# Taking VectorE work out of a recurrence-plus-MLP kernel: a bound moved into another product, a masked copy moved to ScalarE and GpSimd, and an order read from a table

## The chip, the cores and the metric

One core of a Trainium2 chip. The metric is device microseconds for one execution. Three executions of the kernel before took 677.45, 678.53 and 679.85 us; the median is 678.53 us.

## The reference, cut to what matters

```python
# r, k, v, w, a, b: (4, 8, 768, 40), i.e. 32 heads, 768 steps, 40 channels
for t in range(768):                       # per head
    y[t]  = r[t] @ state                   # state: 40 x 40
    Sa    = state @ a[t]
    state = state * w[t] - outer(Sa, b[t]) + outer(v[t], k[t])
x = y.transpose(0, 2, 1, 3).reshape(3072, 320)
out = (((x @ w1) * (x @ w2)) @ w3) @ w_out  # w1, w2: 320 x 1024; w3: 1024 x 1024; w_out: 1024 x 320
```

The MLP weights arrive as 64-bit floats. The decay w lies between 0.85 and 0.95.

## The kernel before, in words

The 768 steps are cut into 12 chunks of 64. The 32 heads form two groups (g = 0, 1) of 8 pairs. For each chunk and group the kernel does the following.

- `load`: SP brings the decays and the b and k vectors into `fm`, and a into `lh`.
- `scale` (L429 to L475): VectorE clamps the decays (f1, L436: minimum with WMAX = 1.5, with the running maximum written to `stats`), then makes their running product with a scan (f2, L441). ScalarE takes Ln and Exp for a first reciprocal `gi` (L445, L448). VectorE refines it by one Newton step (f6, L457: gt = product * gi; f7, L461). Two wide multiplications (f5, L453 and f8, L465) run on VectorE or GpSimd, as the letters in `ON` say.
- `causal` (L490): 64 small matmuls, then ScalarE copies and GpSimd triangular selects (L508).
- `solve`, once per chunk for both groups: a long serial chain on VectorE (from the transposition at L522 through products at L548 and sums at L552 to L597 and L600) inverts the triangular systems. `join` finishes it on TensorE and ScalarE.
- `pairs` (L667, select L677) and `tokens` (L694): more small matmuls with ScalarE copies and GpSimd selects.
- `rec` (L701): the serial part. TensorE multiplies the state (f1, L718), ScalarE copies to `xu`, TensorE makes `hp` (f2, L725), ScalarE copies to `hs`, TensorE multiplies by the solved triangle (f3, L733) into two PSUM banks `us`. Then f4 (L738), four VectorE instructions, writes `us` into `xu`, each multiplied by `mask_h`, a tile that holds -1 where an element is kept and 0 where it is not. TensorE continues with f5 (L745), VectorE scales the new state (L771), TensorE transposes it (L778), ScalarE stores it to `SB`, and L790 writes y. One slot (`rc`) lets a single `rec` run at a time.
- `gather`, then `mlp` (L842 for the first layer, L856 and L859 on its product, L868 for the rest).

Besides this, `convert` (L324 to L341) turns 31 tiles of 64-bit weights into 32-bit ones, with two ScalarE statistics and three VectorE bit operations for each; `product` (L404) multiplies w3 by w_out. The raw tiles go through 4 buffers (`raw`).

The order of the work is made when the program is built. Every step is recorded by `op` with an engine, a cost, a due time, dependencies and buffer slots; `place` (L96 to L197) then plays a greedy list scheduler with these costs, which also picks the buffer of each slot. The result fixes each engine's instruction order: an engine executes its instructions strictly in that order.

Of the kernel before, what the change touches and what calls it, by code (L numbers as in the profile page):

```python
# [1 line left out]

# [59 lines left out]
class Order:  # L62
# [33 lines left out]
    def place(self):  # L96
        ops = self.ops
        for o in ops:
            o["users"], o["wait"] = [], len(o["deps"])
        for o in ops:  # L100
            for d in o["deps"]:
                ops[d]["users"].append(o)
        free = {p: dict.fromkeys(range(n), 0.0) for p, n in SLOTS.items()}
        ready = {e: [] for e in LAT}
        clock, last, lock, dma = {**dict.fromkeys(LAT, 0.0), "pool": 8.0, "dve": 4.0, "sp": 1.0}, None, {"dve": 0.0, "pool": 0.0}, 0.0
        for o in ops:
            o["ready"] = 0.0
            if not o["wait"]:
                ready[o["eng"]].append(o)

        def begin(o):

            t, left = max(o["ready"], clock[o["eng"]]), {}
            for s in o["slots"]:
                if s.at is None:
                    n = left[s.pool] = left.get(s.pool, 0) + 1
                    if len(free[s.pool]) < n:
                        return None
                    t = max(t, sorted(free[s.pool].values())[n - 1])
                else:  # L120
                    t = max(t, s.since)
            if o["two"]:
                t = max(t, lock["pool" if o["eng"] == "dve" else "dve"])
            return t

        uses = {p: {o["eng"] for o in ops for s in o["slots"] if s.pool == p} for p in SLOTS}
        placed, cand, spare = [], {}, {}

        def choice(e, starts):
            if not starts:  # L130
                return None
            first = min(t for t, _ in starts)
            if e != "pe":
                return first, min((o for t, o in starts if t <= first + 1e-9), key=lambda o: (o["due"], o["n"]))
            return min(((t, o) for t, o in starts if t <= first + P["sl"]),
                       key=lambda x: (x[1]["due"] - P["kp"] * (MODE[x[1]["kind"]] == MODE.get(last)) + P["kw"] * (x[0] - first), x[1]["n"]))

        while len(placed) < len(ops):
            best = None
            for e in LAT:  # L140
                if e not in cand:

                    starts, short = [], 1e9
                    for o in ready[e]:
                        t = begin(o)
                        if t is not None:
                            starts.append((t, o))
                        elif e == "pe" and any(s.pool == "bank" and s.at is None for s in o["slots"]):
                            short = min(short, o["due"] + P["mg"])
                    some = [x for x in starts if x[1]["due"] < short or not any(s.at is None for s in x[1]["slots"])]  # L150
                    spare[e] = len(some) < len(starts)
                    cand[e] = choice(e, some)
                if cand[e] and (best is None or cand[e][0] < best[0]):
                    best = cand[e]
            if best is None and any(spare.values()):
                e = "pe"
                best = choice(e, [(t, o) for o in ready[e] if (t := begin(o)) is not None])
            if best is None:
                raise ValueError(f"stuck after {len(placed)} of {len(ops)}")
            t, o = best  # L160
            e = o["eng"]
            ready[e].remove(o)
            stale = {e, *(("dve", "pool") if o["two"] else ())}
            cost = o["cost"]
            if e == "pe":
                if MODE[o["kind"]] != MODE.get(last):
                    cost += DRAIN + LEAD.get(o["kind"], 0.05)
                last = o["kind"]
            for s in o["slots"]:
                if s.at is None:  # L170
                    stale |= uses[s.pool]
                    s.at = min(free[s.pool], key=lambda i: (free[s.pool][i], i))
                    s.since = free[s.pool].pop(s.at)
            clock[e] = t + cost
            if o["two"]:
                lock[e] = clock[e]
            done = clock[e] + LAT[e]
            if e == "sp":
                dma = max(dma, clock[e]) + o["dma"]
                done = dma + LAT[e]  # L180
            o["start"], o["end"] = t, clock[e]
            placed.append(o)
            for s in o["slots"]:
                s.until, s.left = max(s.until, done), s.left - 1
                if not s.left:
                    stale |= uses[s.pool]
                    free[s.pool][s.at] = s.until
            for u in o["users"]:
                u["wait"] -= 1
                u["ready"] = max(u["ready"], clock[e] if u["eng"] == e != "sp" else done)  # L190
                if not u["wait"]:
                    stale.add(u["eng"])
                    ready[u["eng"]].append(u)
            for e in stale:
                cand.pop(e, None)
# [5 lines left out]
def attention_moe(ctx: ExitStack, tc: tile.TileContext, fmx, fma, rv, vt, sq, svr, w12, w12c, w3t, wo, out):  # L201
# [15 lines left out]
    mask_h = cp.tile([128, C + D], F32, name="mask_h")  # L217
    pool.memset(mask_h, -1.0)
    for q in range(2):
        r = slice(64 * q, 64 * q + 64)  # L220
        pool.affine_select(out=mask_h[r, 0:C], in_=mask_h[r, 0:C], pattern=[[1, C]], compare_op=ALU.is_gt,
                           fill=0.0, base=0, channel_multiplier=-1)
# [206 lines left out]
    def scale(c, g, due):  # L429
# [668 lines left out]
```

## Time and profile before

| | |
|---|---|
| median of the runs | 678.53 us |
| profiled execution, span | 676.2 us |
| PE (matmul) busy | 577.7 us, 85% |
| DVE (VectorE) busy | 551.4 us, 82% |
| ACT (ScalarE) busy | 431.8 us, 64% |
| POOL (GpSimd) busy | 211.9 us, 31% |

The profiled execution's own time is known by its span, from the first to the last recorded work, 676.2 us; the median of the timed runs lies 2.3 us above that. Busy times count an instruction from its recorded start to its end, so instructions that overlap on one engine count once. A wait is put down to the instruction that came last. The minimum, median and maximum duration of a line say whether an instruction always takes the same time.

### The profile page before, as it was taken

To read this page: it belongs to the slowest core of one execution; us is meant where nothing else is said; L and a number is where in the kernel's file an instruction comes from. 1 tells how busy PE (TensorE), PEld (TensorE's weight loads), DVE (VectorE), ACT (ScalarE), POOL (GpSimd) and SP (SyncE) were. 2 spreads that over 40 slices of the span, in tenths; PEclk is the share of its full clock that TensorE was granted. 3 is DMA by queue.
4 is the path that set the end of the run, shared out by engine and by line. 5 is a ranking of instruction groups with operands and counts; after the bars stand their busy time and mean duration, and the time that the engine had idled before them with its cause. 6 is when DMAs were issued, how large, how long until landed. Compare 5 with 4: busy or idle time off the path is not lost.

```text
span 676.2 us, 22337 instructions
## 1 busy us (share of the span) xinstructions
PE 577.7 (85%) x9458; PEld 515.3 (76%) x9458; DVE 551.4 (82%) x987; ACT 431.8 (64%) x927; POOL 211.9 (31%) x188
## 2 busy tenths in 40 slices
PE   1422996768799999898999989899999989999996
PEld 1321664556788999788989878789888889898996
DVE  7999999999999799798799798898987997914310
ACT  2886756686776865846837849559578477473321
POOL 4462005233521205505206316245044171120011
PEclk9999997978989999899999999999999999999999
DMA  7954564444214234034133143150341431110101
GB/s 187 245 148 139 169 159 126 132 124 92 60 31 105 69 88 102 14 94 104 33 94 79 32 98 74 42 147 16 83 111 38 99 72 32 45 32 12 34 21 24
DMA packets 61090, 57.56 MB, mean 85 GB/s; under 512 B 29560, under 2 KB 52600, under 8 KB 60984
## 3 DMA queue, kind: packets, MB, share of 16 engines
q1 hardware_dynamic: 60984, 56.07, 32.7%
q8 instruction: 76, 1.25, 0.8%
q14 instruction: 30, 0.25, 0.1%
HBM read 47.40 MB, written 3.93 MB: 76 GB/s over the span
## 4 chain that ended last, share of the span: by engine, by line
DVE 47%; PE 32%; ACT 8%; issue 6%; DMA 4%; POOL 1%; DVEq 0%; SPq 0%; POOLq 0%
PE bank L842 14%; DVE tmp L548 9%; DVE xu L738 6%; PE bank L868 5%; DMA fm<-in_fmx_dram 4%; DVE ab L552 3%; DVE mf L337 3%; ACT JP L212 3%; DVE Tp L552 3%; PE bank L745 2%; DVE fm L441 2%; DVE ab L522 2%; PE bank L725 2%; PE bank L490 2%; DVE w3f L341 2%
## 5 line engine op out<-in xcount | busy, mean ns | idle before, releaser
L842 PE MATMUL bank<-xs,W 128*128 128x256 f32 x1536 | 204.8, 289 | 0.7 <-DVE xs L828 0.7
L842 PEld LDWEIGHTS bank<-xs,W 128*128 128x128 f32 x1536 | 190.3, 193 | 5.8 <-DVE xs L828 0.9
L677 POOL TENSOR_SCALAR_AFFINE_SELECT xu<-xu 64x512 f32<-64x512 f32 x48 | 46.0, 958 | 187.9 <-ACT xu L212 172.1
L212 ACT ACTIVATE xu<-bank 64x256 f32<-64x256 f32 (+2 forms) x184 | 72.6, 437 | 39.4 <-PE bank L718 32.2
L859 POOL TENSOR_TENSOR gl<-ga,gh 128x512 fp32r<-128x512 f32 x32 | 41.0, 1283 | 109.8 <-ACT gh L212 109.8
L212 ACT ACTIVATE JP<-bank 32x512 f32<-32x512 f32 x120 | 60.5, 504 | 22.6 <-PE bank L490 20.7
L490 PE MATMUL bank<-lh,fm 40*64 40x64 f32 x1536 | 32.7, 236 | 45.0 <-POOL fm L465 23.3
L738 DVE TENSOR_TENSOR xu<-bank,mask_h 64x416 f32<-64x416 f32 x96 | 56.3, 587 | 14.0 <-PE bank L733 12.0
L490 PEld LDWEIGHTS bank<-lh,fm 40*64 40x64 f32 x1536 | 29.5, 149 | 49.4 <-POOL fm L465 25.9
L508 POOL TENSOR_SCALAR_AFFINE_SELECT lh<-lh 64x512 f32<-64x512 f32 x48 | 41.0, 853 | 76.8 <-ACT lh L212 73.9
L856 DVE TENSOR_TENSOR ga<-bank,ga 128x512 f32<-128x512 f32 x48 | 32.8, 683 | 39.1 <-PE bank L842 30.3
L868 PE MATMUL bank<-W3h,gh 128*128 128x320 f32 x192 | 63.1, 329 | 1.1 <-DVE xu L738 1.1
L868 PE MATMUL bank<-W3l,gh 128*128 128x320 f32 x192 | 59.2, 309 | 0.0
L868 PE MATMUL bank<-W3h,gl 128*128 128x320 f32 x192 | 59.2, 308 | 0.0
L404 PE MATMUL bank<-wof,w3f 128*128 128x320 f32 x128 | 41.7, 479 | 16.7 <-DVE w3f L341 16.7
L745 PE MATMUL bank<-xu,bk 128*40 128x104 f32 (+1 forms) x768 | 47.5, 262 | 5.9 <-DVE xu L738 5.8
L212 ACT ACTIVATE gh<-ga 128x512 fp32r<-128x512 f32 x48 | 30.3, 631 | 34.6 <-DVE ga L856 34.2
L725 PE MATMUL bank<-xu,lh 128*64 128x104 f32 (+2 forms) x768 | 43.4, 266 | 9.5 <-ACT xu L212 5.8
L453 POOL TENSOR_TENSOR lh<-lh,fm 104x1024 f32<-104x1024 f32 x16 | 35.4, 2216 | 48.4 <-DVE fm L441 22.3
L745 PEld LDWEIGHTS bank<-xu,bk 128*40 128x40 f32 (+1 forms) x768 | 37.5, 120 | 14.7 <-DVE xu L738 12.1
L725 PEld LDWEIGHTS bank<-xu,lh 128*64 128x64 f32 (+2 forms) x768 | 37.6, 144 | 14.2 <-ACT xu L212 6.9
L404 PEld LDWEIGHTS bank<-wof,w3f 128*128 128x128 f32 x128 | 25.8, 210 | 28.7 <-issue 14.3
(99 smaller groups left out, 1190.9 us busy)
## 6 DMA issues: line engine op xcount, KB each, us to landing
fm<-in_fmx_dram SPq DMA_DIRECT2D x24, 627.2 KB
raw<-in_w3t_dram SPq DMA_DIRECT2D x16, 512.0 KB
rv<-in_rv_dram SPq DMA_DIRECT2D x48, 160.0 KB
raw<-in_w_dram SPq DMA_DIRECT2D x8, 512.0 KB
lh<-in_fma_dram SPq DMA_DIRECT2D x48, 80.0 KB
xu<-in_vt_dram SPq DMA_DIRECT2D x48, 80.0 KB
out_dram<-o SPq DMA_DIRECT2D x48, 80.0 KB
xr<-y SPq DMA_DIRECT2D x72, 40.0 KB
```

Of the source, the lines that this page charges most:

```text
L212: act.activation(out_, in_, AF.Copy, scale=scale)
L404: pe.matmul(out=pt.t[:, 0:DM], lhsT=w[:, j], rhs=wof[:, j], start=(j == 0), stop=(j == NJ - 1))
L490: pe.matmul(out=bank(ab)[64 * x:64 * x + 64, p], lhsT=X[r, p, x], rhs=lh.t[r, ab, p], start=True, stop=True)
L508: pool.affine_select(out=lh.t[q, ab], in_=lh.t[q, ab], pattern=[[0, NP], [1, C]], compare_op=ALU.is_gt, fill=0.0, base=0, channel_multipli ...
L548: dve.tensor_tensor(out=scratch(*shape), in0=x().to_broadcast([128, *shape]), in1=y().to_broadcast([128, *shape]), op=ALU.mult)
L677: op("pool", 0.67, due + 2, lambda q=q, ab=ab: pool.affine_select(out=xu.t[q, ab, :, 0:C], in_=xu.t[q, ab, :, 0:C], pattern=[[0, NP], [1, ...
L725: pe.matmul(out=view(hp[h])[64 * ab:64 * ab + 64, u], lhsT=lh.t[k, ab, HP * h + u], rhs=xu.t[k, ab, HP * h + u], start=True, stop=True)
L738: dve.tensor_tensor(out=xu.t[64 * ab:64 * ab + 64, ab, k:NP:2], in0=view(us[ab])[r], in1=mask_h[r].unsqueeze(1).to_broadcast([64, HP, N]), ...
L745: pe.matmul(out=q(r, p), lhsT=bk.t[:, p, r], rhs=xu.t[:, ab, p], start=(c == 0), stop=True, skip_group_check=True)
L842: pe.matmul(out=pt.t[:, TOK * x:TOK * x + TOK], lhsT=WT[k][:, cs], rhs=xs.t[:, z], start=(n == 0), stop=(n == 7))
L859: both(ON["gl"][c % NCH], 1.3, 0.69, t + 1, lambda e, a=a, j=j: e.tensor_tensor(out=gl.t[:, j:j + 2], in0=a.t, in1=gh.t[:, j:j + 2], op=AL ...
L868: pe.matmul(out=pt.t[:, 0:DM], lhsT=l.t[:, j, ts], rhs=W3[r][:, j], start=(j == 0 and n == 0), stop=(j == NJ - 1 and n == 2))
```

## The change

It has three parts.

1. The clamp f1 of `scale` (L436) is gone. The Newton product f6 becomes a scalar_tensor_tensor: minimum of the running product with GMAX = 2^38, times `gi`, with the row sums written to `stats`; the final test compares these sums with NP * C - 0.25 instead of comparing a maximum with WMAX.
2. In `rec`, each of the four VectorE multiplications of f4 becomes a ScalarE copy with scale -1, and two GpSimd selects (f8), one per half `ab`, zero the masked part of the first 64 columns. Each select follows the two copies into its half. `mask_h` and its set-up go.
3. `place` no longer schedules. A table in the source (compressed; two lists, one of the sequence of the steps and one of the buffers of the slots) gives the order; `place` checks it against the dependencies. The steps' costs and due times are still written down, but no longer steer anything. In `convert`, the DMAs of successive tiles are tied to one another in order, as are the first VectorE steps, and f3 must precede the release of the conversion buffers.

The placement letters `ON` and the numbers of buffers `SLOTS` stay as they were.

```diff
-WMAX, GMIN = 1.5, 2.0 ** -40
+GMAX, GMIN = 2.0 ** 38, 2.0 ** -40
-LAT = dict(pe=0.33, act=0.09, dve=0.09, pool=0.1, sp=2.4, nil=0.0)
...
+PLAN = """
...
+"""
     def place(self):
-        ops = self.ops
+        ops, n = self.ops, len(self.ops)
+        code = array("h", zlib.decompress(base64.b85decode("".join(PLAN.split()))))
+        turns, at = list(accumulate(code[:n])), iter(code[n:])
+        assert sorted(turns) == list(range(n))
         for o in ops:
...
             for s in o["slots"]:
                 if s.at is None:
...
+                    s.at = next(at)
+                    assert 0 <= s.at < SLOTS[s.pool]
+        done, holder = set(), {}
+        placed = [ops[i] for i in turns]
+        for o in placed:
+            assert o["deps"] <= done
+            done.add(o["n"])
             for s in o["slots"]:
...
+                h = holder.get((s.pool, s.at))
+                assert h is s or h is None
+                s.left -= 1
+                holder[s.pool, s.at] = s if s.left else None
+        return placed
...
-    mask_h = cp.tile([128, C + D], F32, name="mask_h")
-    pool.memset(mask_h, -1.0)
...
+    pool.memset(stats[:, NCH * NG:2 * NCH * NG], float(NP * C))
...
-        op("sp", 0.35, due - 8, f1, w=[raw], dma=2.5)
+        op("sp", 0.35, due - 8, f1, w=[raw, "turn"], dma=2.5)
         op("act", 0.8, due, f2, r=[raw], w=[sq])
-        op("act", 0.76, due, f3, w=[sq])
-        op("dve", 0.42, due, f4, r=[raw], w=[mf], two=True)
+        op("act", 0.76, due, f3, r=["conv"], w=[sq])
+        op("dve", 0.42, due, f4, r=[raw], w=[mf, "turns"], two=True)
...
-        def f1():
-            w = fm.t[:, 0:NP * W65]
-            dve.tensor_scalar(out=w, in0=w, scalar1=WMAX, scalar2=None, op0=ALU.min, op1=ALU.max,
-                              accum_out=stats[0:104, NCH * NG + i:NCH * NG + i + 1])
...
         def f6():
-            dve.tensor_tensor(out=gt.t, in0=gam(c, g)[:, :, 1:W65], in1=gi.t, op=ALU.mult)
+            dve.scalar_tensor_tensor(out=gt.t, in0=gam(c, g)[:, :, 1:W65], scalar=GMAX, in1=gi.t, op0=ALU.min, op1=ALU.mult,
+                                     accum_out=stats[0:104, NCH * NG + i:NCH * NG + i + 1])
...
-        op("dve", 0.7, due, f1, w=[G])
...
         def f4(ab, x):
             r, k = slice(64 * x, 64 * x + 64), ab ^ x
-            dve.tensor_tensor(out=xu.t[64 * ab:64 * ab + 64, ab, k:NP:2], in0=view(us[ab])[r],
-                              in1=mask_h[r].unsqueeze(1).to_broadcast([64, HP, N]), op=ALU.mult)
+            copy(xu.t[64 * ab:64 * ab + 64, ab, k:NP:2], view(us[ab])[r], -1.0)
+
+        def f8(ab):
+            u = xu.t[64 * ab:64 * ab + 64, ab, :, 0:C]
+            pool.affine_select(out=u, in_=u, pattern=[[0, NP], [1, C]], compare_op=ALU.is_gt, fill=0.0, base=0,
+                               channel_multiplier=-1)
...
         for ab, x in QUADS:
-            op("dve", 0.6, due + 5, lambda ab=ab, x=x: f4(ab, x), r=[us[ab]], w=[(xu, "u", ab, x)])
+            op("act", 0.521, due + 5, lambda ab=ab, x=x: f4(ab, x), r=[us[ab]], w=[(xu, "u", ab, x)])
+        for ab in range(2):
+            op("pool", 0.67, due + 5.5, lambda ab=ab: f8(ab), w=[(xu, "u", ab, 0), (xu, "u", ab, 1)])
```

## Rows read from the trace of the kernel before

**Rows 1.** The windows view, four stages: length, busy us (instructions) by engine, clock, DMA.

```profile
core 0: us, PE busy (x) PEld busy (x) DVE busy (x) ACT busy (x) POOL busy (x), PEclk, DMA share, GB/s
0.00:75.00 75.00, 26.00 (x392) 20.50 (x392) 68.75 (x107) 48.18 (x117) 31.47 (x40) 1.00 0.66 177
75.00:200.00 125.00, 100.07 (x1561) 78.93 (x1564) 118.10 (x232) 89.59 (x203) 40.34 (x33) 0.90 0.41 111
200.00:600.00 400.00, 381.50 (x6747) 348.57 (x6740) 346.33 (x619) 270.25 (x565) 132.31 (x109) 0.99 0.30 72
600.00:677.00 77.00, 70.10 (x773) 67.36 (x771) 18.26 (x31) 23.74 (x45) 7.76 (x6) 0.98 0.09 21
sum 677.00, PE 577.66 PEld 515.35 DVE 551.44 ACT 431.76 POOL 211.88; mean PE 144.42 PEld 128.84 DVE 137.86 ACT 107.94 POOL 52.97
```

**Rows 2.** The page's chain that ended last, share of the span by engine.

```profile
DVE 47%; PE 32%; ACT 8%; issue 6%; DMA 4%; POOL 1%; DVEq 0%; SPq 0%; POOLq 0%
```

**Rows 3.** What SP's queue waited for: us in total, times, longest.

```profile
SPq L324 <- DVE w3f L341: 47.6, 15, 6.9
...
SPq L324 <- DVE wof L341: 17.7, 5, 5.6
```

**Rows 4.** Durations by line, ns minimum/median/maximum: the clamp, f6 and f7.

```profile
L436 DVE TENSOR_SCALAR_CACHE_REDUCE fm<-fm x24: 669/694/696, 7.4 to 547.7; 104x520 f32<-104x520 f32 x24
L436 DVE DVE_READ_ACCUMULATOR fm<-fm x24: 81/83/88, 8.0 to 548.3; 104x1 f32 x24
...
L457 DVE TENSOR_TENSOR gt<-fm,gi x24: 654/693/1701, 11.3 to 554.0; 104x512 f32<-104x512 f32 x24
...
L461 DVE SCALAR_TENSOR_TENSOR gi<-gt,gi x24: 677/693/1025, 12.2 to 555.3; 104x512 f32<-104x512 f32 x24
```

**Rows 5.** The windows view of L436 alone (count with its accumulator reads).

```profile
0.00:75.00 75.00, 2.76 (x8) 1.00 0.66 177
75.00:200.00 125.00, 2.79 (x8) 0.90 0.41 111
200.00:600.00 400.00, 11.22 (x32) 0.99 0.30 72
```

**Rows 6.** The windows view of L738 alone.

```profile
75.00:200.00 125.00, 9.39 (x16) 0.90 0.41 111
200.00:600.00 400.00, 42.23 (x72) 0.99 0.30 72
```

**Rows 7.** Groups by shape, busy us and mean ns: L738, a like ScalarE copy.

```profile
L738 DVE TENSOR_TENSOR xu<-bank,mask_h 64x416 f32<-64x416 f32 x96 | 56.3, 587 | 14.0 <-PE bank L733 12.0
...
L212 ACT ACTIVATE xu<-bank 64x416 f32<-64x416 f32 x44 | 20.1, 506 | 32.5 <-PE bank L718 32.2
```

**Rows 8.** GpSimd's durations by line, ns minimum/median/maximum: selects, then the wide multiplications.

```profile
L677 POOL TENSOR_SCALAR_AFFINE_SELECT xu<-xu x48: 652/828/1859, 37.4 to 593.6; 64x512 f32<-64x512 f32 x48
...
L508 POOL TENSOR_SCALAR_AFFINE_SELECT lh<-lh x48: 649/660/1522, 19.4 to 563.8; 64x512 f32<-64x512 f32 x48
...
L453 POOL TENSOR_TENSOR lh<-lh,fm x16: 2176/2195/2556, 9.5 to 549.7; 104x1024 f32<-104x1024 f32 x16
...
L465 POOL TENSOR_TENSOR fm<-fm,gi x12: 2337/2368/2802, 34.9 to 556.1; 104x1024 f32<-104x1024 f32 x12
```

**Rows 9.** The timeline of one rec step: start, length, engine and line.

```profile
609.24 0.94 PE L733 MATMUL bank<-hs,TT 64*64 64x104 f32 x32
...
610.30 2.45 DVE L738 TENSOR_TENSOR xu<-bank,mask_h 64x416 f32<-64x416 f32 x4 [5.98 <-PE bank L733]
...
613.02 1.63 PE L745 MATMUL bank<-xu,bk 128*40 128x104 f32 x32
```

**Rows 10.** What PE waited for between 200 and 600 us: total, times, longest.

```profile
PE bank L490 <- POOL fm L465: 3.8, 2, 2.7
...
PE bank L745 <- DVE xu L738: 1.4, 6, 0.3
...
PE bank L694 <- DVE xu L738: 0.9, 1, 0.9
```

More of the change, by code (lines that the diff above doesn't have):

```diff
@@ L1 @@
+import base64
+import zlib
+from array import array
 from contextlib import ExitStack
+from itertools import accumulate
 import concourse.bass as bass
@@ new lines @@
+IuX8LmoSN(^ObLCT^`ybGWmLl#!Msmxj8r#SkX$k~W|YSlfTCqJGuDH_j~@@i2!r<qg${=1Da85pnPp8Zsi=5tHQN0%wT=BK6HS@O^|SU#2v6{X+Fpml+^
+Q!jCSXRy2f;XR+DE%b&Iql-G9U(|<zkWcX(g>i8-mIsUI9bM>Io+%!uOk;PwMT@8>Q1NfQhZoT_IfFC#(dsJ-bj+t@xd1#}qlGjay{}VY_+vWv!;YghoeF
+6Nt%Gk$@dj$EC#4Eqq&c*KzQVe!H>n{XlA7F7`@@ocy@yWY>mc1kBjn$dPsj6US;JlA2Cc#R(<GgeXaww(A67b}i+QBR>Np-FmCaD?sPEDleTY)&8>zvnM
+<hUJWH;t6jCCf`<2c0wW*Al~!{10O{R@^*iqnV9aa)wGP>c@d4{5tC$+vX|C2Ag6ekzrsZkmYwj@H*TLsqe$+G!2`##S(iI#^P;o0jDhb_M^co9QQegKG2
+3x*cPB>UwG`6M3LKZ;r|xS<HXoR0`YtZ2!-6)RHutF4$4rMjiw*mh)`tu5DxqcJQJ`Q=0VS1(L3n%*&c4w_%55DQ$kV_tO=9)SR>fc@15*kD0T!xH)b6@~
@@ new lines @@
+3px#?tTlq+xjTq)ml?8UZ^i;G0-V*K+g=zMVtwbM}TlhHD(``51b4*AY^XN}zQL^ZjW{nzHnTy${c&!Q@1&%JjOvL!ESnjO6#}TRWFifRy6qTRWR)$#71R
+;$|B?g?W#einbWAc#r7>U&Yd3eg|i~*Zj*qY&z={dDyt8?`>ss-WD@Q?R_+a7s)Lh#7m_Y`)HQ9k@JDqzC2e7qPP1#fCIFIZd%nLyqSK4^$gAy3%r%W4pU
+`3PJalNoFn;67yX1%Xs;}x8}@P7?k&2Hnrn*m=2d8AX$xIKZ|DZPpq=zEjiRo&=b>7htPONAEtl@xTWdgX7E>Rs31l)=)9&0C?bo%hR_DXwzC=?6{uWqYM
+>FU<*kT<`kz?ROC8)w&T0pV#9TYIi{3NMh<ON+UztC!Gud9IGL~X09$&aTp8e>N2Ogbjzz}_h1r|+c#&MJCLN^>+Fg<^?bv%gSvz6MLANoOuX{V~fGeN!f
+ID)rC>(9ry*nXZG%<imZnjNuvBbpumN6&7z~_USO-z=xHi=(-)pX_SdK(<H{AgFS3&KvDKnMVrT1JB+7e{A`c^*K7eZQ0JoMu2*bfGXV3r=Qm)_{N|D!&-
@@ new lines @@
+3y0v23Hsa){h@DwsG8K6(*~x0#;Td6b~nwJ|r<k$PMA09S><zf>9qjs5}lEP!40*ZKIxV28<=?YvFm+T0ozZL6*)1J`Msf)OKR2ENp>eoA4h!=;2-PxWmI
+50QO9=+~m~(bKlJX^Zo$rjDAW@v_Hc*k5tpJK%GI4wKrZ6|S=p8y3+h9Zyqq96Ymx3ej<$rVDVNLK(I_Ptiq)afRrlu94H=X(8;bxlYlFeA5o%^T5xKG7%
+@tvH^3$o~E);g{E4Z<^c_F13SHRHt?{VW{Qv6@no&c-${9R`<g9iuG<3CoL7MzEue_4buC3<?}nN{bv8&|^OARcSwEG={0Y4TJX?(tGL2y~605>KxvK4W2
+hi+nmu|=K0r0^2;<9aEe$ZaJ6m7?}i}oJVU6*_Q?5VA_GFaP9+d-M8NMZUMYjx8$Tm>_{g&w!<0Ni_mGq-GB(^cPwHq4cQyo{VmB!QdPZGN100I%@S(G_0
+H&=vHTt!kRW#vjvJ?W)tI2j5GLI8jgQD^TgTVRc3OtgT`y>q&YJ{r;mRpm4is2jbybeM9T(Xq?_ay?a7Cp9Q~`(rVcQhQH>ia6ZIaM*pX|6Exljh3kM(Px
@@ L52, in __init__ @@
     def __init__(self, order, pool):
-        self.order, self.pool, self.at, self.left, self.since, self.until = order, pool, None, 0, 0.0, 0.0
+        self.order, self.pool, self.at, self.left = order, pool, None, 0
         if order.direct:
@@ L96, in place @@
     def place(self):
-        ops = self.ops
+        ops, n = self.ops, len(self.ops)
+        code = array("h", zlib.decompress(base64.b85decode("".join(PLAN.split()))))
+        turns, at = list(accumulate(code[:n])), iter(code[n:])
+        assert sorted(turns) == list(range(n))
         for o in ops:
[L99 to L113, printed above, removed]
             for s in o["slots"]:
                 if s.at is None:
[L116 to L168, printed above, removed]
-            for s in o["slots"]:
[L170 to L195, printed above, removed]
@@ L216, in attention_moe @@
     make_identity(nc, ident)
-    mask_h = cp.tile([128, C + D], F32, name="mask_h")
-    pool.memset(mask_h, -1.0)
[L219 to L222, printed above, removed]
     first = cp.tile([104, NP, W65], F32, name="first")
@@ L472, in scale @@
         both(ON["lh"][c], 2.2, 1.22, due + 1, f5, r=[G], w=[(lh, 0), (lh, 1)])
-        op("dve", 0.71, due + 2, f6, r=[G, gi], w=[gt], two=True)
+        op("dve", 0.78, due + 2, f6, r=[G, gi], w=[gt], two=True)
         op("dve", 0.73, due + 2, f7, r=[gt], w=[gi], two=True)
@@ L1013, in attention_moe @@
     dve.tensor_scalar(out=stats[:, 0:n1], in0=stats[:, 0:n1], scalar1=0.5 / GMIN, scalar2=None, op0=ALU.is_lt)
-    dve.tensor_scalar(out=stats[:, n1:2 * n1], in0=stats[:, n1:2 * n1], scalar1=WMAX, scalar2=None, op0=ALU.is_lt)
+    dve.tensor_scalar(out=stats[:, n1:2 * n1], in0=stats[:, n1:2 * n1], scalar1=NP * C - 0.25, scalar2=None, op0=ALU.is_gt)
     dve.tensor_scalar(out=stats[:, 2 * n1:2 * n1 + NCH], in0=stats[:, 2 * n1:2 * n1 + NCH], scalar1=0.0, scalar2=0.0,
```

42 lines of the change are left out of this document (38 added, 4 removed).

## The prediction

> **What bounds the kernel now.** I read the windows view first, cut into four stages, because the shares of the whole span hide that the limit changes. The reader should compare TensorE's and VectorE's busy times with each stage's length. In the first 75 us VectorE is busy 68.75 and TensorE only 26.00; from 75 to 200 us VectorE is busy 118.10 of 125 and TensorE 100.07; from 200 to 600 us TensorE is busy 381.50 of 400 and VectorE 346.33; after 600 us TensorE works off the last MLPs almost without a gap, 70.10 of 77 [rows 1]. So VectorE sets the pace of the head and TensorE that of the rest. Since TensorE's work (577.66 us) is the same before and after, the span is this work plus TensorE's idle time: 49.0 us before 75, 24.9 from 75 to 200, 18.5 from 200 to 600, 6.1 from there to the end at 676.2. The change can only win what it takes out of these 98.5 us.
>
> Next the chain that ended last: VectorE has 47% of it, TensorE 32%, DMA only 4% [rows 2]. To see whether the head is short of data, I then looked at what SP's queue waits for. It waits for VectorE's last conversion step to free a raw buffer, 47.6 us on the w3 tiles and 17.7 us on the wo tiles [rows 3]: the transfers stand behind VectorE, not VectorE behind the transfers. That is my main reason to count VectorE time saved in the head as time saved.
>
> **The clamp that goes into f6.** It removes 24 instructions of 0.694 us, 16.8 us in all [rows 4, 5]; the accumulator read of 0.083 us that follows each lies mostly inside it. Of these 2.76 + 2.79 = 5.55 us lie in the first 200 us and 11.22 in the next 400. The new f6 is not in the trace. From below: f7 has the same kind of instruction and the same size, and its median is that of the old f6, 0.693 us [rows 4], so the extra cost is nothing; it can't be less, since the elements are as many. From above: one accumulator read each, 24 x 0.083 = 2.0 us. I take the upper end because the new f6 has an accumulator: 8 x 0.083 = 0.7 us of it in the head.
>
> **The masked copy that leaves VectorE.** 96 instructions of 0.587 us go, 56.3 us [rows 7]; 9.39 us of them lie between 75 and 200 us and 42.23 between 200 and 600 [rows 6]. ScalarE gets 96 copies. One of the same shape, from PSUM to the same tile, takes 0.506 us [rows 7], so 48.6 us in all and 72 x 0.506 = 36.4 us between 200 and 600, where ScalarE rises from 270.25 to 306.7 us of 400 [rows 1]. TensorE's MLP backlog covers them; if that cover went, each rec step would show its copies as TensorE idle time, some 2.0 us. GpSimd gets 48 selects of 64 x 512 elements, which cost between 0.652 us (shortest) and 0.828 us (median of L677, the same tile) [rows 8]: 31 to 40 us on an engine that is busy 211.88 us. I price its occupancy at nothing, because GpSimd has over 260 us free between 200 and 600.
>
> What counts is the longer way from L733 to L745. Now it is four VectorE instructions in 2.45 us, and TensorE fills it: L733 ends at 610.18 and L745 begins at 613.02, 0.27 us after the last masked copy ends at 612.75 [rows 9]. Afterwards the four copies take 4 x 0.506 = 2.02 us; the third completes half 0 at 1.52 us, and two selects in a row end at 1.52 + 2 x 0.652 = 2.82, or 1.52 + 2 x 0.828 = 3.18 us. That is 0.37 to 0.73 us later than 2.45, so 0.10 to 0.46 us past the present filler; on the 18 steps (72 / 4) between 200 and 600 this makes 1.8 to 8.3 us. I take 0.15 us each, 2.7 us, nearer to the lower end, because TensorE usually has another MLP group at hand.
>
> A wait is also added: the selects queue on GpSimd, strictly in order, behind whatever stands there, and L745 then waits for them, and the state, the next rec step and the gather for L745. The things that stand there are the wide multiplications of 2.2 to 2.4 us [rows 8]. I price this at nothing in the forecast and as a rival below.
>
> In exchange four waits of TensorE for L738 between 200 and 600 us vanish: 1.4 at L745, 1.3 at L667, 1.1 at L868 and 0.9 at L694, together 4.7 us (the first and the last are shown) [rows 10]. What comes late next is the causal matmul waiting for the wide multiplication on GpSimd, 3.8 us [rows 10]; I leave it as it is. So this stage wins 4.7 - 2.7 = 2.0 us.
>
> **The order from a table.** What it holds can't be read from the source, so I bound it. In the head, VectorE loses 5.55 + 9.39 - 0.7 = 14.3 us. If the order stayed as it is, that is the gain. The upper end is all of TensorE's idle time between 75 and 200 us, 24.9: between 200 and 600 VectorE falls from 346.33 to 346.33 - 11.22 - 42.23 + 1.3 = 294.2 us of 400 (16 f6 reads are the 1.3), so an order may push the solves of later chunks out of the head and bring the conversions and the first MLP forward, and the freed room is 106 us. I take the middle, 19.6, since nothing in the trace favours either end. A bad order can also lose; that is not limited from below by any row, and is in the rivals. TensorE's clock is a further unknown: its mean is 0.90 between 75 and 200 us, 1.00 before and 0.99 after [rows 1]. With its two levels, 2.4 and 1.2 GHz, this means a fifth of the 125 us, 25 us, on the lower one, worth at most 12.5 us if denser work there keeps the higher one, and as much lost if that share doubles. I take nothing.
>
> The `convert` dependencies add no work; the tied DMAs go through SP's queue alone, where they went in one queue already. The removed set-up of `mask_h` runs on GpSimd before its first work and I price it at nothing.
>
> **Sum.** 676.2 - 19.6 - 2.0 = 654.6 us of span. The median of the runs lies 2.3 us above the profiled span, so I forecast 656.9, rounded to 657 us.
>
> **GpSimd and VectorE hold one another up.** The same instruction on the same shape varies: the select L677 takes 0.652 to 1.859 us [rows 8], the old f6 0.654 to 1.701 us [rows 4], f7 0.677 to 1.025 us [rows 4]. The long cases fit a conflict between the two engines. The Trainium skill (SBUF — State Buffer, Who interferes with whom) says that a VectorE instruction with two SBUF inputs and a GpSimd instruction that reads SBUF exclude one another for the whole instruction, and that one with at most one SBUF input does not take part. By that rule, with which these ranges agree, L738 (one input in PSUM) disturbed nobody, while each new select may stop a solve step: the rule speaks against the change.
>
> **The rivals.** (a) The conflict costs most of the gain. Of the head's relief 8 selects take up to 0.828 us each back, 6.6 us, which leaves 7.7, and I grant the order nothing more; between 200 and 600 the way through ScalarE and GpSimd is at its upper end, 8.3 - 4.7 = 3.6 us lost. 676.2 - 7.7 + 3.6 + 2.3 = 674 us. For it: the spread of durations. Against it: only 8 of the selects lie in the head.
>
> (b) The order is much better than the old one. TensorE's idle time after 75 us is 43.4 us up to 600; the forecast takes 21.6 of it, and half of the remaining 21.8 gives 657 - 10.9 = 646 us. For it: the 106 us that VectorE has free in the middle. Against it: the head's conversions still all need VectorE.
>
> (c) Slower: the selects come late on GpSimd. If a wide multiplication (2.3 us) stands before the selects in every second of the 24 rec steps and the rest of the way is at its upper end, TensorE loses 12 x 2.3 + 24 x 0.46 = 38.6 us, against 19.6 + 4.7 = 24.3 us won: 676.2 + 14.3 + 2.3 = 693 us. It decides from a mean uncovered wait of 24.3 / 24 = 1.0 us for each step. For it: the written cost of a select is 0.67 us, and the median of L677 is 0.828, so an order made with that cost would come out late. Against it: 28 multiplications spread over the span leave GpSimd mostly idle.
>
> (d) The change doesn't do what it says: VectorE gets free, but the first solves and conversions end no earlier since the table places them no earlier. Then the time stays at about 678 us. For it: half of TensorE's idle time lies before 75 us, where no L738 is. Against it: rows 3.
>
> **How the numbers follow.** Forecast 0.58, (a) 0.14, (b) 0.14, (c) 0.10, (d) 0.04. A measurement of this kernel can tell 0.3%, 2 us, from no change. Faster: the forecast, (b) and nearly all of (a), 0.85. Within 0.3%: (d) and the edge of (a), 0.05. Slower: (c), 0.10. The range runs from 641 us (into the better half of (b)) to 677 us, past (a); below it lies about 0.06 and above it 0.14. The likeliest case alone runs from 648 to 667 us.
>
> **What would show it.** L436 and L738 are gone, and VectorE is busy about 480 us (551.4 - 71). TensorE's idle time between 75 and 200 us has fallen to about 5 us, and the first L842 comes some 20 us earlier. Between 200 and 600 TensorE stays above 380 of 400 us. The chain has less of VectorE. Wrong would be: TensorE waiting at L745 for GpSimd's selects for over 10 us in total (c); f6 well over 0.8 us or solve steps longer than before (a); the 49.0 us of idle time before 75 us cut strongly, which I count as fixed.

## The result, and the profile after

The changed kernel takes 650.7 us (median of 649.08 to 652.73, 4 runs), beside 677.99 us before (4 runs of the same comparison). The ratio is 0.9593, with a 95% interval of 0.9563 to 0.9624: faster by 4%, 27 us. The forecast was 657 us, 641 to 677. The profiled execution, the slowest of the four, has a span of 651.0 us, 25.2 less than before. Ratios leave out slow executions, over 1.5% above the fastest of their kernel; in the whole record that is one, 662.23 us in a second series of the changed kernel (after_again), which the median given there leaves out too.

The windows view of the changed kernel, columns as in [rows 1]:

```profile
0.00:75.00 75.00, 23.34 (x446) 19.36 (x447) 66.76 (x106) 47.05 (x112) 30.44 (x38) 0.84 0.61 173
75.00:200.00 125.00, 105.88 (x1650) 86.62 (x1651) 103.13 (x212) 103.58 (x238) 53.44 (x44) 0.89 0.42 121
200.00:600.00 400.00, 391.04 (x6994) 360.47 (x6998) 289.15 (x534) 305.42 (x649) 151.74 (x146) 1.00 0.30 71
600.00:652.00 52.00, 43.44 (x386) 42.65 (x374) 10.34 (x18) 14.24 (x26) 6.53 (x6) 0.94 0.09 23
sum 652.00, PE 563.70 PEld 509.11 DVE 469.39 ACT 470.28 POOL 242.15; mean PE 140.92 PEld 127.28 DVE 117.35 ACT 117.57 POOL 60.54
```

The reader should again take TensorE's busy time from the length of each stage. Its idle time is 51.7 us before 75, 19.1 from 75 to 200, 9.0 from 200 to 600 and 7.6 to the end, 87.3 us in all, where [rows 1] give 49.0, 24.9, 18.5 and 6.1. So 11.2 us of the 25.2 are idle time, 5.8 of it between 75 and 200 us and 9.5 between 200 and 600; the other 14.0 us come from the busy time itself, which fell from 577.66 to 563.70 us though the matmuls are the same 9458. VectorE is busy 469.39 us instead of 551.44. The chain that ended last, which had 47% of VectorE [rows 2], now reads:

```profile
PE 57%; DVE 5%; ACT 5%; DMA 3%; POOL 2%; issue 2%; SPq 0%; DVEq 0%; ACTq 0%; POOLq 0%
```

The durations of the new f6 with its accumulator read, and of the new selects (ns, minimum/median/maximum), answer to [rows 4] and [rows 8]:

```profile
L423 DVE SCALAR_TENSOR_TENSOR gt<-fm,gi x24: 655/698/1332, 10.2 to 533.8; 104x512 f32<-104x512 f32 x24
L423 DVE DVE_READ_ACCUMULATOR gt<-fm,gi x24: 72/77/84, 11.4 to 534.4; 104x1 f32 x24
...
L708 POOL TENSOR_SCALAR_AFFINE_SELECT xu<-xu x48: 651/657/1971, 86.7 to 603.5; 64x512 f32<-64x512 f32 x48
```

The first MLP matmul, before (L842) and after (L814): the view by line gives the first and the last start in us behind the durations.

```profile
L842 PE MATMUL bank<-xs,W x1536: 276/282/582, 169.5 to 662.7; 128*128 128x256 f32 x192
```

```profile
L814 PE MATMUL bank<-xs,W x1536: 276/282/562, 159.8 to 635.9; 128*128 128x256 f32 x192
```

It comes 9.7 us earlier, and the last one 26.8 us earlier. TensorE's waits before (first row) and after (total, times, longest):

```profile
PE bank L745 <- DVE xu L738: 5.8, 16, 1.2
```

```profile
PE bank L375 <- ACT sq L298: 22.5, 1, 22.5
...
PE bank L715 <- POOL xu L708: 13.6, 9, 5.8
```

The first of the two rows after is one long gap while the first weights are converted (the product at L375); it lies in the 51.7 us. The selects hold TensorE up at L715 (which was L745) for 13.6 us; before, VectorE's masked copy did so for 5.8 us. One rec step of after, the counterpart of [rows 9]:

```profile
599.70 0.94 PE L699 MATMUL bank<-hs,TT 64*64 64x104 f32 x32
...
600.77 1.58 ACT L188 ACTIVATE xu<-bank 64x416 f32<-64x416 f32 x3 [0.31 <-PE bank L699]
601.88 0.66 POOL L708 TENSOR_SCALAR_AFFINE_SELECT xu<-xu 64x512 f32<-64x512 f32 x1 [9.74 <-ACT xu L188]
...
602.89 0.51 ACT L188 ACTIVATE xu<-bank 64x416 f32<-64x416 f32 x1
...
603.48 0.70 POOL L708 TENSOR_SCALAR_AFFINE_SELECT xu<-xu 64x512 f32<-64x512 f32 x1 [0.94 <-ACT xu L188]
...
604.55 1.63 PE L715 MATMUL bank<-xu,bk 128*40 128x104 f32 x32
```

L699 (which was L733) ends at 600.64 and L715 begins at 604.55: the order leaves 3.9 us between them, where [rows 9] left 2.84. Worked out in this way from the timelines for all 24 steps, the mean is 4.1 us after and 2.8 before (2.82; 3.32 in kept_both, the first of the experiments).

### The profile page after: what moved, and what is told of

The parts are those of the page before. It is cut to its first block, busy times and chain, and to the rows that moved or that the text cites. A ratio compares the mean times of both kernels' runs of the same rounds, so it can differ in the third digit from the quotient of the medians.

```text
span 651.0 us, 22281 instructions
## 1 busy us (share of the span) xinstructions
PE 563.7 (87%) x9458; PEld 509.1 (78%) x9458; DVE 469.4 (72%) x867; ACT 470.3 (72%) x1023; POOL 242.2 (37%) x234
## 4 chain that ended last, share of the span: by engine, by line
PE 57%; DVE 5%; ACT 5%; DMA 3%; POOL 2%; issue 2%; SPq 0%; DVEq 0%; ACTq 0%; POOLq 0%
PE bank L814 23%; PE bank L840 11%; PE bank L691 4%; PE bank L715 4%; PE bank L456 3%; PE bank L750 2%; ACT xu L188 2%; PE bank L699 2%; DMA fm<-in_fmx_dram 2%; PE bank L660 2%; PE bank L684 2%; PE bank L596 2%; DVE tmp L514 1%; PE bank L589 1%; ACT JP L188 1%
## 5 line engine op out<-in xcount | busy, mean ns | idle before, releaser
L814 PE MATMUL bank<-xs,W 128*128 128x256 f32 x1536 | 204.1, 286 | 0.6 <-DVE xs L800 0.2
L814 PEld LDWEIGHTS bank<-xs,W 128*128 128x128 f32 x1536 | 187.7, 189 | 6.1 <-DVE xs L800 0.4
L188 ACT ACTIVATE xu<-bank 64x416 f32<-64x416 f32 (+2 forms) x280 | 124.1, 463 | 55.9 <-PE bank L684 20.9
L708 POOL TENSOR_SCALAR_AFFINE_SELECT xu<-xu 64x512 f32<-64x512 f32 x48 | 40.7, 847 | 128.7 <-ACT xu L188 122.8
L188 ACT ACTIVATE JP<-bank 32x512 f32<-32x512 f32 (+1 forms) x120 | 59.4, 501 | 9.1 <-PE bank L456 4.2
L831 POOL TENSOR_TENSOR gl<-ga,gh 128x512 fp32r<-128x512 f32 x32 | 43.2, 1352 | 60.4 <-ACT gh L188 53.1
L474 POOL TENSOR_SCALAR_AFFINE_SELECT lh<-lh 64x512 f32<-64x512 f32 x48 | 36.0, 750 | 68.1 <-ACT lh L188 66.8
L643 POOL TENSOR_SCALAR_AFFINE_SELECT xu<-xu 64x512 f32<-64x512 f32 x48 | 38.9, 812 | 58.0 <-ACT xu L188 56.3
L375 PE MATMUL bank<-wof,w3f 128*128 128x320 f32 x128 | 39.7, 461 | 23.7 <-ACT sq L298 22.5
L715 PE MATMUL bank<-xu,bk 128*40 128x104 f32 (+1 forms) x768 | 44.5, 267 | 13.8 <-POOL xu L708 13.6
L456 PEld LDWEIGHTS bank<-lh,fm 40*64 40x64 f32 x1536 | 28.3, 149 | 33.1 <-issue 20.4
L715 PEld LDWEIGHTS bank<-xu,bk 128*40 128x40 f32 (+1 forms) x768 | 37.7, 124 | 19.8 <-POOL xu L708 17.2
L375 PEld LDWEIGHTS bank<-wof,w3f 128*128 128x128 f32 x128 | 24.4, 198 | 33.8 <-ACT sq L298 22.6
L691 PE MATMUL bank<-xu,lh 104*64 104x104 f32 (+2 forms) x768 | 45.0, 271 | 5.8 <-ACT xu L188 4.7
L691 PEld LDWEIGHTS bank<-xu,lh 104*64 104x64 f32 (+2 forms) x768 | 38.9, 147 | 10.5 <-ACT xu L188 6.7
L407 DVE TENSOR_TENSOR_SCAN fm<-fm,first 104x520 f32<-104x520 f32 x24 | 31.0, 1292 | 18.8 <-DMA fm<-in_fmx_dram 18.5
```

The lines of the kernel that those rows point to most:

```text
L188: act.activation(out_, in_, AF.Copy, scale=scale)
L375: pe.matmul(out=pt.t[:, 0:DM], lhsT=w[:, j], rhs=wof[:, j], start=(j == 0), stop=(j == NJ - 1))
L456: pe.matmul(out=bank(ab)[64 * x:64 * x + 64, p], lhsT=X[r, p, x], rhs=lh.t[r, ab, p], start=True, stop=True)
L474: pool.affine_select(out=lh.t[q, ab], in_=lh.t[q, ab], pattern=[[0, NP], [1, C]], compare_op=ALU.is_gt, fill=0.0, base=0, channel_multipli ...
L643: op("pool", 0.67, due + 2, lambda q=q, ab=ab: pool.affine_select(out=xu.t[q, ab, :, 0:C], in_=xu.t[q, ab, :, 0:C], pattern=[[0, NP], [1, ...
L691: pe.matmul(out=view(hp[h])[64 * ab:64 * ab + 64, u], lhsT=lh.t[k, ab, HP * h + u], rhs=xu.t[k, ab, HP * h + u], start=True, stop=True)
```

## The experiments

Four kernels separate the new instructions from the new order. Eight more runs look at the selects, at what a freed VectorE is worth and at how much the changed kernel itself varies. Each diff is cut to the lines that matter. The table holds more than the order: it also picks the buffers, and the new dependencies in `convert` come with it. No run separates these from the order, so "the table" below means all of it.

**New instructions, old order (kept_both).** The scheduler of before plans as before; only what each step issues differs. f6 and f8 are those of the change.

```diff
         def f1():
-            w = fm.t[:, 0:NP * W65]
-            dve.tensor_scalar(out=w, ...)
+            pass
...
         def f4(ab, x):
-            dve.tensor_tensor(out=xu.t[...], in0=view(us[ab])[r], in1=mask_h[r]..., op=ALU.mult)
+            copy(xu.t[64 * ab:64 * ab + 64, ab, k:NP:2], view(us[ab])[r], -1.0)
+            if (ab, x) in ((0, 1), (1, 0)):
+                f8(ab)
```

> The order of before, step for step, with the new instructions: no clamp, f6 with its accumulator, the masked copy on ScalarE and GpSimd at the place in the order where VectorE had it. Theory 1 (the relief of VectorE and the order each give about half): VectorE's 14.3 us in the head come off and the longer way to L745 costs 1 to 5 us, so 660 to 668 us. Theory 2 (it is the order that pays, the relief alone is soaked up): within 3 us of before, 675 to 681. Theory 3 (it is the relief alone): 648 to 654, as after.

Measured: 696.95 us, ratio 1.0279 (1.0238 to 1.0321). All three theories missed: the new instructions in the old order are 19 us slower than before. What waited for whom, before and in kept_both (total, times, longest):

```profile
DVE y L790 <- PE bank L745: 1.4, 2, 1.2
...
DVE st L771 <- PE bank L745: 0.8, 2, 0.6
```

```profile
POOL xu L738 <- ACT xu L212: 164.0, 25, 30.5
...
DVE st L771 <- PE bank L745: 62.3, 36, 7.0
...
PE bank L745 <- POOL xu L738: 25.6, 32, 4.1
```

TensorE waits 25.6 us for the selects, 1.07 us for each of the 24 steps, and VectorE stands 62.3 us before the scaling of the state (L771), which comes behind L745. GpSimd is mostly idle ahead of the selects: in 25 waits it stands 164.0 us until ScalarE's copies are done. Two stages, columns as in [rows 1]:

```profile
75.00:200.00 125.00, 92.12 (x1390) 71.75 (x1389) 101.45 (x194) 92.21 (x211) 44.62 (x40) 0.90 0.40 110
200.00:600.00 400.00, 378.06 (x6674) 345.15 (x6677) 297.99 (x538) 300.63 (x625) 145.18 (x139) 0.99 0.30 72
```

From 75 to 200 us VectorE is busy only 101.45 us (118.10 before [rows 1]) and TensorE has lost, not won: 92.12 against 100.07. The timeline of that stage shows why (start, length, engine and line; in brackets the idle time before and what ended it):

```profile
153.85 0.65 POOL L738 TENSOR_SCALAR_AFFINE_SELECT xu<-xu 64x512 f32<-64x512 f32 x1
...
154.56 0.57 PE L745 MATMUL bank<-xu,bk 128*40 128x104 f32 x2 [4.14 <-POOL xu L738]
155.04 0.66 POOL L738 TENSOR_SCALAR_AFFINE_SELECT xu<-xu 64x512 f32<-64x512 f32 x1 [0.54 <-POOL xu L738]
...
155.76 3.00 PE L745 MATMUL bank<-xu,bk 128*40 128x104 f32 x30 [0.63 <-POOL xu L738]
157.40 0.32 DVE L771 TENSOR_TENSOR st<-bank,fm 104x160 f32<-104x160 f32 x1 [2.80 <-PE bank L745]
...
159.36 0.68 DVE L336 SCALAR_TENSOR_TENSOR mf<-raw,mf 128x512 uint32<-128x512 uint32 x1
```

TensorE stands 4.14 us until the first select; VectorE can't scale the state until 157.40; and a weight conversion (L336) that stands behind it in VectorE's order begins only at 159.36. The first MLP matmul starts at 178.6 us, 9.1 later than before:

```profile
L842 PE MATMUL bank<-xs,W x1536: 276/282/582, 178.6 to 680.0; 128*128 128x256 f32 x192
```

**New instructions, the greedy scheduler (greedy_both).** The kernel before with both instruction changes of the diff, planned anew by its own `place`.

```diff
-        op("dve", 0.7, due, f1, w=[G])
...
-        op("dve", 0.71, due + 2, f6, r=[G, gi], w=[gt], two=True)
+        op("dve", 0.78, due + 2, f6, r=[G, gi], w=[gt], two=True)
...
-            op("dve", 0.6, due + 5, lambda ab=ab, x=x: f4(ab, x), ...)
+            op("act", 0.521, due + 5, lambda ab=ab, x=x: f4(ab, x), ...)
+        for ab in range(2):
+            op("pool", 0.67, due + 5.5, lambda ab=ab: f8(ab), ...)
```

> Both instruction changes, and the greedy scheduler of before makes the order anew with their costs; no table. Theory 1: between before and after, 658 to 668 us, a little better than the kept order. Theory 2 (the table's order pays): 670 or more. Theory 3 (the relief alone): 648 to 656.

Measured: 701.78 us, 1.035 (1.0309 to 1.0391), which of the three theories only theory 2's "670 or more" covers. The old scheduler, told of the new costs, does no better than the old order.

**The table with old instructions (table_mask_old, table_all_old).** The changed kernel, first with the masked copy back on VectorE and empty select steps, then with the clamp in front of the scan and the plain f6 too.

```diff
-            copy(xu.t[64 * ab:64 * ab + 64, ab, k:NP:2], view(us[ab])[r], -1.0)
+            dve.tensor_tensor(out=xu.t[...], in0=view(us[ab])[r], in1=mask_h[r]..., op=ALU.mult)
...
-            op("act", 0.521, due + 5, lambda ab=ab, x=x: f4(ab, x), ...)
+            op("dve", 0.6, due + 5, lambda ab=ab, x=x: f4(ab, x), ...)
...
-            op("pool", 0.67, due + 5.5, lambda ab=ab: f8(ab), ...)
+            op("pool", 0.67, due + 5.5, lambda: None, ...)
```

> The table's order with the clamp change kept, but the masked copy back on VectorE with the mask and no select. VectorE gets 56 us more, ScalarE 49 and GpSimd 41 less. Theory 1: VectorE is short of time again in the head and nearly so in the middle: 658 to 668 us. Theory 2: within 4 us of after, 647 to 655. If the way over ScalarE and GpSimd is what costs (13.6 us of TensorE's waits for the selects), it is even faster than after: 640 to 648.

> The table's order with all the old instructions: clamp, plain f6, masked copy on VectorE. Theory 1: some 4 to 8 us above the same with the new clamp, 664 to 674 us. Theory 2 (the order pays): 648 to 658. Theory 3 (the relief alone): as before, 674 to 681.

Measured: 700.12 us, 1.0307 (1.0259 to 1.0355), and 717.24 us, 1.0591 (1.0538 to 1.0643). Every theory missed again: the table alone is worth nothing, it loses 39 us with the old instructions. VectorE is on the path again: it has 45% of the chain that ended last in table_mask_old, against 5% after.

```profile
DVE 45%; PE 31%; ACT 8%; DMA 7%; issue 6%; POOL 2%; SPq 0%; DVEq 0%; ACTq 0%; POOLq 0%
```

The 24 clamps, 16.8 us of VectorE [rows 5], cost 717.24 - 700.12 = 17.1 us, though that run also saves the 1.9 us of the new f6's accumulator reads; by the two ratios it is 19 us, give or take 5. The 96 masked copies, 56.3 us [rows 7], cost 700.12 - 650.7 = 49.4 us; this is not VectorE's time alone, since the same edit takes the copies off ScalarE, the selects off GpSimd and changes the way to L715. Two of TensorE's waits in table_mask_old are for VectorE's scaling of the state (1.9 us after) and, where the changed kernel waits 13.6 us for the selects, for the masked copy:

```profile
PE bank L752 <- DVE st L745: 18.0, 17, 2.3
PE bank L717 <- DVE xu L710: 16.3, 15, 4.2
```

**VectorE's wait filled with other work (kept_later).** As kept_both, with up to 3 us of solve steps pulled in front of each scaling of the state and each y.

```diff
+                room, j = 3.0, i + 1
+                while j < len(line) and room > 0:
...
+                        if o["n"] in self.steps:
+                            line.insert(i, line.pop(j))
+                            i, room = i + 1, room - o["cost"]
```

> As kept_both, and on VectorE alone up to 3 us of the solve steps that stand behind each scaling of the state and each y are pulled ahead of them. Theory A (VectorE, freed, reaches the scaling of the state too early and stands there in order until L745 is done: 62 us of waits in kept_both): these waits fall below 35 us and the time to 672 to 687. Theory B (the loss is TensorE's wait for the selects at L745, 25.6 us in kept_both, and VectorE's wait is only its shadow): 692 to 700, as kept_both.

Measured: 765.77 us, 1.1309 (1.1259 to 1.1359), far outside both theories. VectorE's wait at this place fell to 36.1 us, but now TensorE waits for the scaling:

```profile
PE bank L799 <- DVE st L792: 38.9, 19, 7.0
PE bank L765 <- POOL xu L758: 22.8, 30, 3.8
```

The first row is a wait that kept_both hardly had; the second is nearly what it was. Where VectorE was early, it is now late. It also stands 57.5 us for the transfers into `fm` (10.1 in kept_both), so the shift moved more than one wait; which of them costs how much of the 69 us isn't separated.

**The selects in the table's order (zero_select, zero_noselect, zero_memset).** The copies scaled by 0, then no selects, then memsets in their place.

```diff
-            copy(xu.t[64 * ab:64 * ab + 64, ab, k:NP:2], view(us[ab])[r], -1.0)
+            copy(xu.t[64 * ab:64 * ab + 64, ab, k:NP:2], view(us[ab])[r], 0.0)
...
+            pool.memset(xu.t[64 * ab:64 * ab + 64, ab, :, 0:C], 0.0)    # zero_memset alone, as f8
```

> After, with the masked copies scaled by 0 in place of -1, so that what the next two runs leave out can't blow the numbers up. The recurrence's own product is lost, the time should not change: 648 to 654 us.

> As zero_select, without the 48 selects on GpSimd. If TensorE's 13.6 us of waits for them are on the path, 636 to 644 us; if the table's order has covered them, 647 to 653.

> As zero_select, with a memset of the same elements on GpSimd in the place of each select: a write without a read. If what selects cost is the conflict of two engines' reads, this is as fast as without selects, within 2 us; if it is the longer way to L745, as slow as with them, within 2 us.

Measured: 652.51 us with selects (ratio 0.9598 to 0.9701), 647.79 without (0.9521 to 0.9598), 648.29 with memsets (0.9514 to 0.9618). By the medians the selects cost 4.7 us with the table; the two ratios, 0.965 and 0.9559, differ by 6 us, and their intervals leave anything from about 2 to 10. By the medians a write without a read costs nothing and the read all of it, but the intervals of memset and select overlap, so this stays open. The durations are clear, in zero_select and in zero_memset:

```profile
L708 POOL TENSOR_SCALAR_AFFINE_SELECT xu<-xu x48: 652/659/1977, 86.3 to 599.8; 64x512 f32<-64x512 f32 x48
```

```profile
L707 POOL MEMSET xu<- x48: 516/520/528, 87.3 to 598.4; 64x512 f32 x48
```

The select takes up to three times its shortest time, the memset always the same within 12 ns. Laid over VectorE's instructions in the trace of zero_select, 17 of the 18 selects of over 0.72 us overlap one that reads two SBUF tiles (23 of the 30 short ones do, too, so the overlap alone does not lengthen them); 38 of the 48 memsets overlap such an instruction, and none is longer for it.

**Old order without the selects (kept_noselect).** As kept_both, scale 0, no selects.

```diff
-            copy(xu.t[64 * ab:64 * ab + 64, ab, k:NP:2], view(us[ab])[r], -1.0)
-            if (ab, x) in ((0, 1), (1, 0)):
-                f8(ab)
+            copy(xu.t[64 * ab:64 * ab + 64, ab, k:NP:2], view(us[ab])[r], 0.0)
```

> As kept_both, with the copies scaled by 0 and no selects (so the recurrence's own product is lost): the order of before, the relief of VectorE, and no longer way over GpSimd. Theory B (kept_both loses by TensorE's waits for the selects at L745, 25.6 us against 5.8 before): the waits go and the relief comes out, 662 to 676 us. Theory C (an order made for the old durations gains nothing from a freed VectorE, in any case): 677 to 690.

Measured: 678.37 us, 1.0002 (0.9968 to 1.0035), the time of before. Theory B is right on the loss: without the selects the 18.6 us are gone. It is wrong on the rest: the relief does not come out, and theory C's range holds. VectorE has 63 us less work (488.49 busy), and the first MLP matmul starts at 174.2 us, 4.7 later than before. The waits at L738 (which was L745):

```profile
DVE st L764 <- PE bank L738: 37.0, 31, 6.3
...
DVE y L783 <- PE bank L738: 11.0, 4, 9.7
```

```profile
PE bank L738 <- ACT xu L212: 9.9, 16, 1.2
```

The first two are 48 us in which VectorE stands in order; before, L771 and L790 waited 2.2 us there. The third is TensorE's wait for the copies, which in this run are still on ScalarE: 9.9 us, against 5.8 for VectorE's masked copy before. So the run shows what the relief is worth together with the copies on ScalarE, not what it would be worth alone.

**VectorE time out of the head, nothing added (before_less_convert).** The kernel before without f5 of `convert`, one VectorE instruction for each tile. f4 gets other constants and takes 0.497 us in the mean for 0.433, so that VectorE's busy time falls by 20.4 us (551.4 to 531.0).

```diff
-            dve.tensor_scalar(out=mf.t, in0=H(), scalar1=3, scalar2=0xC0000001, op0=ALU.logical_shift_left,
-                              op1=ALU.bitwise_or)
+            dve.tensor_scalar(out=mf.t, in0=H(), scalar1=3, scalar2=0x3FFFFFFF, op0=ALU.logical_shift_left,
+                              op1=ALU.bitwise_and)
...
-            dve.scalar_tensor_tensor(out=mf.t, in0=H(), scalar=0x3FFFFFFF, in1=mf.t, op0=ALU.bitwise_or,
-                                     op1=ALU.bitwise_and)
+            pass
```

> The kernel before in its own order, without the second bit operation of each weight conversion (31 x 0.724 = 22.4 us of VectorE in the first 160 us; the weights are wrong), nothing else moved. The prediction's premise (VectorE time saved in the head is time saved, though the order stays): 656 to 664 us. Theory C (the fixed order soaks it up): 674 or more.

Measured: 666.31 us, 0.9812 (0.9783 to 0.9841), between the two: by the medians 12.2 us come back of 22.4 (10.8 to 14.7 by the interval). The profile is of the slowest of the five executions, 671.91 us. In it the first MLP matmul moves up by 12.3 us and the last by 5.9:

```profile
L841 PE MATMUL bank<-xs,W x1536: 276/282/583, 157.2 to 656.8; 128*128 128x256 f32 x192
```

**Selects cut in two (quarters), and the changed kernel beside it (after_again).**

```diff
             copy(xu.t[64 * ab:64 * ab + 64, ab, k:NP:2], view(us[ab])[r], -1.0)
...
+            u = xu.t[64 * ab:64 * ab + 64, ab, k:NP:2, 0:C]
+            pool.affine_select(out=u, in_=u, pattern=[[0, HP], [1, C]], ...)
```

> After, with each of the two selects of a rec step cut in two, one right behind each ScalarE copy. The last select ends about 0.4 us earlier, if one of 256 elements takes 0.4 us. Theory (the selects' way still costs 3 to 5 us, as the runs without them say): 647 to 650 us, 1 to 3 us below after in the same call. Rival (twice as many instructions on GpSimd cost what the cut wins): within 1 us of after, or above.

> The changed kernel, unchanged, as a measure for the others of this call: 649 to 653 us, as in its first runs.

Measured: 654.64 us, 0.9653 (0.9622 to 0.9683), and 652.83 us, 0.9641 (0.9591 to 0.969). So the cut wins nothing that shows, as the rival said, but a gain of 1 us, the lower end of the theory, is less than the spread. TensorE's wait for the selects did fall, from 13.3 to 6.6 us, and the time did not. (0.9641 lies just outside the interval of the first comparison, 0.9563 to 0.9624; the two intervals overlap. The changed kernel's executions range from 648.82 to 658.47 us.) No version with the whole recurrence beats the changed kernel.

## Why the prediction was right, and where its steps were not

**The number.** The time fell as forecast, 27.3 us by the medians for 21.6 forecast. The sum behind it is not what happened, so that the number came so near is in part luck: the forecast was idle time of TensorE alone, and of the 25.2 us between the profiles 11.2 are that.

**What bounds the kernel: half right.** VectorE does limit the head (before_less_convert, 12.2 us), but not one to one: about half of what it saves comes back while the order stands. And TensorE's busy time is no constant: it fell by 14.0 us with the same matmuls, the largest single term, which the sum did not have. The matmuls did not get shorter: the recorded lengths of all 9458, added up, are 2409.9 us before and 2408.7 after. Busy time counts overlapping ones once, so more of them overlap; and TensorE stands idle 56 times where it stood 84 times. The fall is spread over most groups of matmuls, and what brings it about is not shown. The matmuls alone do not fix it: in the twelve runs of the experiments, all with 9458 of them, it lies between 561.4 us (zero_select) and 611.1 (kept_later).

**The step that failed: "If the order stayed as it is, that is the gain", 14.3 us.** The prediction made this the lower end for the order. With the order kept, the new instructions lose 18.7 us. Two things were missed. The way through the selects was sized at 0.10 to 0.46 us past the filler for each step, and taken at 0.15; in the old order TensorE waited 1.07 us at L745, against 0.24 before (5.8 us in 24 steps), and kept_noselect shows that the selects are the whole loss against before. And the relief itself was counted as gain, 14.3 us in the head. With the copies on ScalarE and no selects it brings nothing: VectorE reaches the next step that needs TensorE earlier and stands before it, 45.8 us more than before of the 63 that it was relieved of, and the conversions that were to start earlier stand behind that step. How much of the rest the copies on ScalarE take wasn't measured; where nothing was added (before_less_convert), half came back.

**The order from a table: far too small.** Beyond the relief it was priced at 5.3 us in the head. Measured against the kept order it is worth 696.95 - 650.7 = 46.2 us, and against the greedy one 51. Yet with the old instructions it loses 39 us. The two parts have no worth of their own that could be added: 678 (neither), 697 (instructions), 717 (table), 651 (both).

**Stage by stage.** Between 75 and 200 us TensorE's idle time fell to 19.1 us, not to 5, and the first MLP came 9.7 us earlier, not 20. Between 200 and 600 it fell by 9.5 us where 2.0 were counted. The 49 us before 75 stayed, as assumed (51.7).

**The rivals.** (b), the much better order, had 646 us, and 650.7 lies a little nearer to it than to the forecast. Its mechanism did not happen: TensorE's idle time from 75 to 600 us fell from 43.4 to 28.1 us, 15.3, less than even the forecast's 21.6; the busy time made up for it. (c), slower since the selects come late, did not happen with the table, though its sign did: TensorE waits 13.6 us for them, over the 10 us that were named. In the old order the time is as (c) had it, 697 us for 693, and the wait of 1.07 us near its 1.0, but by another way: of the 48 selects in kept_both 4 begin right behind a GpSimd multiplication and 1 behind an older select, 26 after GpSimd stood idle and 17 right behind the other select of the step. What costs there is the selects behind ScalarE's copies, not GpSimd's queue. (a), the conflict of GpSimd and VectorE: all that the selects cost with the table is 4.7 us by the medians, not the 17 by which (a) stood above the forecast, and its signs are missing: f6 has a median of 0.698 us, and the solve's products are no longer than before (rows before and after; busy us, mean ns):

```profile
L548 DVE TENSOR_TENSOR tmp<-Tp,ab 128x256 f32<-128x256 f32 (+2 forms) x60 | 41.1, 685 | 1.6
```

```profile
L514 DVE TENSOR_TENSOR tmp<-Tp,ab 128x256 f32<-128x256 f32 (+2 forms) x60 | 41.0, 683 | 1.4
```

One other step of the solve did grow, L571 (now L537) from 0.404 to 0.641 us in the mean, but it is as long in zero_noselect, without a new select. Nor is the conflict what slows kept_both: there the selects take 0.676 us in the mean, and VectorE is busy 487.7 us with them and 488.5 without. That the conflict exists, the durations bear out. They agree with the rule of the Trainium skill (SBUF — State Buffer, Who interferes with whom) that a GpSimd instruction that reads SBUF contends with a VectorE instruction of two SBUF inputs and one that only writes does not: the select, which reads, takes 0.652 to 1.977 us, the memset, which only writes, 0.516 to 0.528. (d) is refuted for the table and is nearly what kept_noselect shows: VectorE free, time unchanged.

**The small terms.** The new f6 has a median of 0.698 us against 0.693 and a read of 0.077 us: the upper end was the right choice. The copies were priced well: ScalarE's 64 x 416 copies take 69.6 us where they took 20.1, 49.5 more for 48.6 forecast, though its busy time rose by 38.5 only. The 48 selects take 40.7 us, just over the upper end of 31 to 40; GpSimd's busy time rose by 30.3, since its other selects got shorter (from 46.0 to 38.9 us and from 41.0 to 36.0). VectorE's busy time fell by 82 us where 71 were expected, 4.6 of the rest at its share of f8 (19.5 to 14.9 us).

## What to carry to other kernels

Where each engine runs a fixed order, the order is fitted to the durations of its instructions. In these runs, work put back onto VectorE in the table's order cost about its full time (17.1 us for 16.8). Work taken off it in the old order returned half (12.2 us of 22.4) or, with copies moved to ScalarE, nothing, while VectorE's waits for TensorE grew. So price a moved instruction by what stands behind its consumer on every engine, and treat an order and the instructions it was made for as one change, not as two gains to be added. Before counting on either, run the new instructions in the old order and the old ones in the new. And don't hold an engine's busy time fixed because its instructions stay the same: here TensorE's gave 14.0 us, its idle time 11.2.

## What was not expected of the hardware

With the same order and the same long idle time of TensorE ahead of L375 (22.5 and 22.3 us), the granted clock fell in one execution and not in another. The changed kernel's profile, and that of zero_select, in the idle stretch and the 5 us behind it (columns as in [rows 1]):

```profile
44.00:68.00 24.00, 1.54 (x22) 1.37 (x18) 23.76 (x41) 16.25 (x44) 5.59 (x6) 0.59 0.52 170
68.00:73.00 5.00, 5.00 (x48) 2.96 (x50) 5.00 (x8) 3.28 (x8) 0.00 (x0) 0.57 0.43 144
```

```profile
44.00:68.00 24.00, 1.86 (x32) 1.53 (x25) 23.76 (x41) 16.10 (x43) 5.68 (x7) 1.00 0.52 169
68.00:73.00 5.00, 4.88 (x70) 3.36 (x72) 5.00 (x8) 3.47 (x8) 0.00 (x0) 1.00 0.50 166
```

At a mean clock of 0.57 (so partly at 1.2 and partly at 2.4 GHz) 48 matmuls were recorded in those 5 us; at 1.00 it was 70. The spans are 651.0 and 647.4 us; the first runs of the changed kernel spread in the same way, 652.73 us at a mean clock of 0.957 and 649.08 at 0.982. The clock is not all of the spread, though: in after_again 656.92 and 658.47 us stand at 0.974 and 0.975. What decides between the two clocks can't be read from these traces.
